# Sparse attention with an FFN: another list of steps for block 0, one exponential for two strided groups, smaller loads of v and q

## The chip, the cores and the metric

The kernel runs on one core of one Trainium2 chip. The metric is the device time of one execution in microseconds (us), as a median of runs. PE is TensorE, DVE is VectorE, ACT is ScalarE, POOL is GpSimd, SP is SyncE, which only issues DMAs here.

## The reference

Eight batches of eight heads, 576 tokens, 64 columns a head, in float32. Heads 0 to 3 attend to the last 32 tokens ("local"), heads 4 to 7 to earlier tokens of the same remainder modulo 32 ("strided"). The result, 4608 tokens of 512 columns, goes through an FFN with a SiLU gate.

```python
rel = pos[:, None] - pos[None, :]
mask_local = (rel >= 0) & (rel < stride)                      # stride = 32
mask_strided = (rel >= 0) & (pos[None, :] % stride == pos[:, None] % stride)
scores = np.where(masks, scale * q @ k.T, -1e9)               # masks by head
attn = np.exp(scores - max); attn = attn / (attn.sum() + 1e-9)
x = attn @ v                                                  # heads side by side
h = x @ w_in                                                  # 512 -> 2048
out = (h * (1.0 / (1.0 + np.exp(-h)))) @ w_out                # 2048 -> 512
```

## The kernel before, in words

**FFN.** The 4608 tokens are nine blocks (k) of 512; the 2048 hidden columns are 16 chunks (fc) of 128. Float32 products are made of a high and a low part each of the operands: for each chunk and block, `hidden` (L617) does twelve products of 128x512 with w_in, `output` (L683) twelve with w_out. The weights' parts are made while block 0 is computed, and stay in SBUF.

**Attention.** A batch is six groups: three local ones of twelve tiles (n = 3 columns of the layout) and three strided ones of 8, 8 and 6 tiles (n = 4, 4, 3). In batch 0 they come in this order, groups 0 to 5; from batch 1 on a local and a strided one in turn. Block 0 needs batch 0, so batch 0's attention stands at the start of the program; two groups later than that (6 to 13) lie inside block 0, and the rest between the chunks of later blocks (`products`, L928), two groups at a time.

**Steps and the list.** The program up to the end of block 0 is a list of steps, written out as text (`PLAN`, L104). `follow` (L163) emits them in the list's order; each engine executes its own instructions in this order, and the semaphores between them follow from what they read and write. A letter after a dot names the engine; without one it is the first of the step's engines. The steps of a group c:

- `kc`: load keys and queries (`load_qk`, L333). In batch 0 this is two DMAs, and for groups 0 to 2 the second one goes through ACT's queue, the others through SP's. Four buffers k0 to k3 serve batch 0, so `k4` waits for S0, `k5` for S1, `k6` for S4. `vc`: load values (L339), in two DMAs on SP.
- `Sc`: scores on PE into two PSUM banks (L384). `Mc`: on DVE, per column and head, minus the scaled and masked score, and its minimum, so that the row's maximum comes out (`peak`, L408). `Ec`: on ACT, one exponential per column and head of 128x64 with the maximum as a bias, and the row sums as a second result (`weigh`, L432). `Rc`: DVE adds 1e-9 and takes the reciprocal (L445).
- `Nc`: multiplies by it (strided groups; DVE or POOL). `Tc`: PE transposes (L460). `Pc`: copies them out of PSUM (ACT or DVE). `Oc`: products with v on PE (L488).
- Local groups go on with `Qc` (DVE divides, L544), `Xc` (PE transposes back, L569) and `Bc` (copy into x); strided ones with `Bc` (sorts into x on ACT, L552).
- From group 6 on, `Vc` (DVE transposes by blocks) takes the place of T and P.

`~n` is n units of 128 columns of products of the identity on PE, without use for the result. `H0c` and `L0c` make the high and low part of x's rows for block 0. A weight's piece i goes through `pi` (load, SP), `ai` (two passes on ACT, L266 and L271), `ji` (DVE, L277), `bi` (high part, DVE or ACT, L318), `di` (low part, DVE or POOL, L322). A chunk fc of block 0 is `h` and `i` (six products each, `hidden`), `t` (tanh, ACT), `g` (DVE), `w` and `l` (high and low part of the gate's output), `o` (twelve products). h0 needs L00, L01 and d0.

**DMAs and semaphores.** DMAs take eight semaphores in turn (DMAHW0 to DMAHW7). A DMA waits until the last one of its own semaphore has landed, on the queue of the engine that issues it, and ACT and SP issue in the order of their instructions.

**Masks.** At the start, POOL builds the local mask of 64 keys and its two variants, those of 96 keys (for the wide form of the scores) and then the strided one (L220 to L240). The wide form (64 queries by 96 keys, half as many products) is used from group 14 on (`WIDE_FROM`).

**End.** `store` (L692) scales the last products out of PSUM, alternately on DVE and ACT, each of 128x512, and SP stores them.

Of the kernel before, what the change touches and what calls it, by code (L numbers as in the profile page):

```python
# [46 lines left out]
WIDE_FROM = 14  # L47
# [8 lines left out]
SPREAD = ()  # L56
# [10 lines left out]
class Group:  # L67
    def __init__(self, local, first, count):
# [4 lines left out]
        self.q0 = [self.rows * t for t in range(count)]  # L73
# [37 lines left out]
N8.D h4 b9.A o1 d9.P t3 g3 h5 M10 p13 E6 p15 v6 b6.D d6.D p12 k7 R6 l2.D o2 a10 j10 a11 j11
b11.D d11.D p17 h6 i4 a8 j8 i5 i6 a13 j13 b13.D w3.A l3.D N6.D V6 b8.A d8.P p14 o3 E10 t4 d13.P
p19 a15 j15 g4 O6 b10.A d10.P p16 t5 g5 h7 b15.D d15.D p21 a12 j12 v8 w4.A l4.D o4 a17 j17
b17.D d17.D p23 R10 i7 w5.A b12.A d12.D p18 a14 j14 a19 j19 B6 t6 g6 S7 k9 h8 l5.D o5 a16 j16
b16.D d16.D p22 V8 k12 M7 i8 t7 g7 O8 h9 v10 N10.P b19.A d19.P w6.A l6.P b14.A d14.D o6 p20 i9
a21 j21 a18 j18 b18.D a23 j23 b23.D w7.A l7.D o7 d23.D p25 a22 j22 b22.D d22.D p24 B8 E7 R7
# [59 lines left out]
def sparse_attention_ffn(ctx: ExitStack, tc: tile.TileContext, kqt, vt, w_in, w_out, out):  # L176
# [44 lines left out]
    for wide, keys in ((False, KW), (True, WIDE)):  # L221
        m = mask(f"mask_local{keys}", keys + 8)
# [4 lines left out]
        masks[wide, ()] = m  # L227
        some = {s for g in GROUPS for s in (g.paired_starts if wide else g.starts) if s}
        for starts in sorted(some):
            first = const.tile([P, keys + 8], F32, name=f"mask{keys}_" + "".join(map(str, starts)))  # L230
            nc.gpsimd.tensor_copy(out=first, in_=m)
            for t in starts:
                keep(first, t * STRIDE, STRIDE, [keys], [1], -STRIDE, 0)
            masks[wide, starts] = first
    m = mask("mask_strided")
# [97 lines left out]
    def load_qk(a):  # L333
        n = max(a.g.nq, a.g.nk)
        ways = (load, nc.scalar.dma_start if a.at < 3 else load)
        for some, way in zip(halved(n, 1 if a.b else 2), ways):
            way(out=kbds[kbd_of(a.b, a.at)][:, :, some], in_=kqt[a.b, a.gi, :, :, some])
# [13 lines left out]
    class Attention:  # L351


        def __init__(self, b, at):
# [24 lines left out]
        def halves(self, banks):  # L379

            n, keys = self.g.n, self.keys
            return [t[:, : n * keys].rearrange("p (c k) -> p c k", k=keys) for t in banks]

        def scores(self, banks=None):  # L384
# [14 lines left out]
            for t, c, rows in self.tiles:  # L399
                for h in range(2):  # L400
                    at = slice(h * D, (h + 1) * D)
                    nc.tensor.matmul(  # L402
                        self.pss[h][rows, c * KW : (c + 1) * KW],
                        kbd[at, 1, g.q0[t] : g.q0[t] + g.rows],
                        kbd[at, 0, g.k0[t] : g.k0[t] + KW], start=True, stop=True,
                    )

        def peak(self):  # L408
# [5 lines left out]
            )  # L414
# [3 lines left out]
            self.inv = rsum.unsqueeze(3).broadcast_to([P, g.n, 2, self.keys])  # L418
            for c in range(g.n):
                for h in range(2):  # L420

                    nc.vector.tensor_tensor_reduce(  # L422
                        out=s_sb[:, c, h], in0=s_ps[h][:, c], in1=self.masks[c][:, : self.keys],
# [4 lines left out]
        def lessen(self):  # L428
            peaks = self.peaks.unsqueeze(3).broadcast_to([P, self.g.n, 2, self.keys])
# [58 lines left out]
        def values(self):  # L488
# [5 lines left out]
            if self.sums_by_pe:  # L494
                for c in range(g.n):
                    at = g.n * D + 2 * c
                    nc.tensor.matmul(
                        self.pso[0][:, at : at + 2], pt[:, c].rearrange("k r q -> k (r q)"), ones,
                        start=True, stop=True,
                    )  # L500
# [210 lines left out]

    def attention_steps(c, due, last=None):
# [6 lines left out]
        cols = max(a.g.nq, a.g.nk)  # L719
        k = add(f"k{c}", {"SP": 2 * P * cols * 4 / RATE}, t0 - 6, [], lambda: load_qk(a),  # L720
# [3 lines left out]
        m = add(f"M{c}", {"DVE": 0.07 + 0.27 * n}, t0 + 1, [s], a.peak, takes=["sm", "sum"],  # L724
# [4 lines left out]
        cost = 0.1 + 0.11 * n if a.spread else 0.667 * n  # L729
# [346 lines left out]
```

## Time and profile before

| | us |
|---|---|
| median of 3 runs | 871.31 (871.29 to 871.56) |
| the profiled execution | 871.88 |
| its span | 870.1 |
| PE busy | 862.5 (99%) |
| DVE busy | 514.1 (59%) |
| ACT busy | 318.7 (37%) |
| POOL busy | 40.3 (5%) |

The profile is one execution: the span goes from the first to the last instruction of the core. PE, DVE, ACT and POOL stand ahead of line, operation, names of the tiles written and read (buffer numbers left out) and sizes; times are us from the span's start, a number in brackets is the engine's idle time ahead of an instruction with what ended it. A 64x64 product of float32 is two matmul records. ACTq and SPq are the queues in which an engine issues DMAs.

### The profile page before, as it was taken

To read this page: it belongs to the slowest core of one execution; us is meant where nothing else is said; L and a number is where in the kernel's file an instruction comes from. 1 tells how busy PE (TensorE), PEld (TensorE's weight loads), DVE (VectorE), ACT (ScalarE), POOL (GpSimd) and SP (SyncE) were. 2 spreads that over 40 slices of the span, in tenths; PEclk is the share of its full clock that TensorE was granted. 3 is DMA by queue.
4 is the path that set the end of the run, shared out by engine and by line. 5 is a ranking of instruction groups with operands and counts; after the bars stand their busy time and mean duration, and the time that the engine had idled before them with its cause. 6 is when DMAs were issued, how large, how long until landed. Compare 5 with 4: busy or idle time off the path is not lost.

```text
span 870.1 us, 17241 instructions
## 1 busy us (share of the span) xinstructions
PE 862.5 (99%) x6809; PEld 707.9 (81%) x6809; DVE 514.1 (59%) x1602; ACT 318.7 (37%) x1070; POOL 40.3 (5%) x68
## 2 busy tenths in 40 slices
PE   8999999999999999999999999999999999999998
PEld 5777788888888888888888888888888888888886
DVE  6999887558556647656655855664762533343333
ACT  7987863315413333333431541333331311131111
POOL 5023320000000000000000000000000000000000
PEclk9999999999999999999999999999999999999999
DMA  9976443202302212220320230221210000000001
GB/s 293 288 251 221 142 157 95 72 2 76 118 1 72 77 50 68 72 77 18 100 73 1 77 117 1 72 76 50 69 29 1 29 20 1 1 27 22 1 1 49
DMA packets 37041, 64.55 MB, mean 74 GB/s; under 512 B 2912, under 2 KB 23776, under 8 KB 36960
## 3 DMA queue, kind: packets, MB, share of 16 engines
q1 hardware_dynamic: 36144, 62.79, 22.3%
q8 instruction: 53, 0.87, 0.4%
q10 hardware_dynamic: 816, 0.66, 0.2%
q14 instruction: 28, 0.23, 0.1%
HBM read 54.00 MB, written 9.44 MB: 73 GB/s over the span
## 4 chain that ended last, share of the span: by engine, by line
PE 92%; DVE 3%; ACT 2%; issue 1%; POOL 1%; POOLq 0%; DVEq 0%; ACTq 0%
PE po L687 44%; PE ps L623 43%; PE ps L526 3%; PE ps L393 1%; PE ps L402 1%; DVE stage L277 1%; DVE sm L422 1%; ACT stage L271 0%; ACT stage L266 0%; POOL mask_local L215 0%; DVE th L655 0%; DVE w L318 0%; ACT xb L566 0%; DVE w L322 0%; ACT sm L439 0%
## 5 line engine op out<-in xcount | busy, mean ns | idle before, releaser
L623 PE MATMUL ps<-xhi,w 128*128 128x512 f32 x1152 | 376.7, 390 | 0.5 <-DVE th L655 0.5
L623 PEld LDWEIGHTS ps<-xhi,w 128*128 128x128 f32 x1152 | 216.2, 188 | 46.0 <-DVE th L655 0.7
L655 DVE SCALAR_TENSOR_TENSOR th<-th,ps 128x512 f32<-128x512 f32 (+1 forms) x147 | 99.2, 675 | 258.6 <-ACT th L633 257.7
L633 ACT ACTIVATE th<-ps 128x512 f32<-128x512 f32 (+1 forms) x147 | 86.7, 590 | 448.3 <-PE ps L623 416.5
L623 PE MATMUL ps<-xlo,w 128*128 128x512 f32 x576 | 224.2, 389 | 0.0
L687 PE MATMUL po<-w,ghi 128*128 128x512 f32 x504 | 156.9, 392 | 0.0
L623 PEld LDWEIGHTS ps<-xlo,w 128*128 128x128 f32 x576 | 108.1, 188 | 22.2
L439 ACT ACTIVATE sm<-sm,sums 128x64 f32<-128x64 f32 (+1 forms) x320 | 109.2, 348 | 2.9 <-DVE sums L422 2.9
L687 PEld LDWEIGHTS po<-w,ghi 128*128 128x128 f32 x504 | 93.7, 188 | 20.0 <-DVE w L322 0.3
L667 DVE TENSOR_TENSOR glo<-th,ghi 128x512 fp32r<-128x512 f32 (+1 forms) x139 | 95.7, 689 | 11.9
L687 PE MATMUL po<-w,glo 128*128 128x512 f32 x252 | 98.4, 390 | 0.4 <-DVE glo L667 0.4
L687 PE MATMUL po<-stage,ghi 128*128 128x512 f32 x288 | 88.8, 389 | 0.0
L486 DVE STREAM_TRANSPOSE pt<-sm 32x192 f32<-32x192 f32 (+1 forms) x168 | 65.8, 392 | 3.0
L687 PE MATMUL po<-v,ghi 128*128 128x512 f32 x216 | 67.5, 394 | 0.0
L663 DVE CAST ghi<-th 128x512 fp32r<-128x512 f32 (+1 forms) x134 | 56.6, 422 | 12.8 <-PE po L687 1.2
L687 PEld LDWEIGHTS po<-stage,ghi 128*128 128x128 f32 x288 | 54.0, 188 | 11.2
L439 ACT ACTIVATION_READ_ACCUMULATOR sm<-sm,sums 128x1 f32 x320 | 61.8, 193 | 0.0
L687 PEld LDWEIGHTS po<-w,glo 128*128 128x128 f32 x252 | 47.3, 188 | 11.1 <-DVE glo L667 1.1
L687 PE MATMUL po<-stage,glo 128*128 128x512 f32 x144 | 56.0, 389 | 0.0
L687 PEld LDWEIGHTS po<-v,ghi 128*128 128x128 f32 x216 | 39.9, 188 | 8.4
L687 PE MATMUL po<-k,ghi 128*128 128x512 f32 x144 | 44.3, 389 | 0.0
L687 PE MATMUL po<-v,glo 128*128 128x512 f32 x108 | 42.0, 389 | 0.0
(77 smaller groups left out, 676.9 us busy)
## 6 DMA issues: line engine op xcount, KB each, us to landing
out<-stage SPq DMA_DIRECT2D x36, 256.0 KB, 2.0
v<-vt SPq DMA_DIRECT2D x21, 384.0 KB, 5.4
stage<-w_out SPq DMA_DIRECT2D x14, 512.0 KB, 4.3
k<-kqt SPq DMA_DIRECT2D x14, 512.0 KB, 4.9
stage<-w_in SPq DMA_DIRECT2D x12, 512.0 KB, 4.4
k<-kqt SPq DMA_DIRECT2D x14, 416.0 KB, 3.9
v<-vt SPq DMA_DIRECT2D x14, 256.0 KB, 5.4
k<-kqt SPq DMA_DIRECT2D x7, 448.0 KB, 3.9
```

Source lines behind the costliest of these rows:

```text
L277: nc.vector.scalar_tensor_tensor(out=upper, in0=upper, scalar=3, in1=lower, op0=ALU.logical_shift_left, op1=ALU.bitwise_or,)
L393: nc.tensor.matmul(self.pss[h][rows, c * WIDE : (c + 1) * WIDE], kbd[at, 1, g.q0[t] : g.q0[t] + 2 * STRIDE], kbd[at, 0, g.k0[t] : g.k0[t] ...
L402: nc.tensor.matmul(self.pss[h][rows, c * KW : (c + 1) * KW], kbd[at, 1, g.q0[t] : g.q0[t] + g.rows], kbd[at, 0, g.k0[t] : g.k0[t] + KW], s ...
L439: nc.scalar.activation(out=self.s_sb[:, c, h], in_=self.s_sb[:, c, h], func=AF.Exp, bias=self.peaks[:, c, h : h + 1], scale=-1.0, accum_ou ...
L486: nc.vector.transpose(out=pt[to, r % 2], in_=src[rows, 1 if self.wide else 1 - r % 2])
L526: nc.tensor.matmul(self.pso[p][h * D : (h + 1) * D, i * size : (i + 1) * size], vbd[at, 2 * i + h], moved, start=True, stop=True,)
L623: nc.tensor.matmul(ph, weight(0, wi, fc)[:, cc * P : (cc + 1) * P], x[xi][cc], start=(cc, n) == (0, 0), stop=(cc, n) == (NP - 1, 2),)
L633: nc.scalar.activation(out=th[:, cols], in_=ph[:, cols], func=AF.Tanh, scale=0.5)
L655: nc.vector.scalar_tensor_tensor(out=th[:, cols], in0=th[:, cols], scalar=1.0, in1=ph[:, cols], op0=ALU.add, op1=ALU.mult,)
L663: copy[engine](out=g[0][:, cols], in_=th[:, cols])
L667: either[engine].tensor_sub(out=g[1][:, cols], in0=th[:, cols], in1=g[0][:, cols].bitcast(F32))
L687: nc.tensor.matmul(po[tt], g[gi][:, cols], weight(1, wi, fc), start=fc == 0 and n == 0, stop=fc == NFC - 1 and n == 2,)
```

## The change

**Steps.** (1) Groups 3 and 4 are in `SPREAD`: a new step `U` on POOL subtracts the maxima from all 128x512 (`lessen`), `E` is one exponential of 128x512 without sums, and `R` begins with a sum on DVE. (2) Groups 0 to 2 are `SHARED`: as neighbouring local tiles share half of their values, only the second half of v's rows is loaded, and a new step `C` on POOL copies the first half from it, within SBUF. (3) Queries of strided groups are packed 59 columns apart instead of 64, and batch 0 loads keys and queries as two DMAs, each with the columns it needs, the queries of groups 0 to 2 through ACT's queue. (4) From group 12 on (`WIDE_FROM`) local scores are wide and strided ones take 54 keys instead of 64 (`seen`), for which POOL sets the rest to zero. (5) The wide masks are built later, in a step `Y0` on POOL, and the strided mask comes third. (6) The very last store is halved: DVE and ACT scale a half each, SP and ACT store one each. (7) Block 0 has a new list.

```diff
-WIDE_FROM = 14
+WIDE_FROM = 12
+SHARED = (0, 1, 2)
-SPREAD = ()
+SPREAD = (3, 4)
-        self.q0 = [self.rows * t for t in range(count)]
+        self.q0 = [(STRIDE if local else STRIDE + HALF) * t for t in range(count)]
 PLAN = """
-k0 k1 k2 k3 v0 ~9 S0 M0 k4 v1 E0 ~1 S1 k5 M1 E1 v2 ~1 S2 M2 E2 R0 ~2 T0 P0.D p0 S3 M3 E3 ~3 T1
...
+k0 k1 v0 C0 v1 ~7 S0 ~1 S1 M0 E0 ~6 T0 P0.A k2 k4 M1 E1 v2 S2 k3 O0 R0 M2 E2 C1 R1 Q0 S4 C2 k5
...
     def load_qk(a):
-        n = max(a.g.nq, a.g.nk)
-        ways = (load, nc.scalar.dma_start if a.at < 3 else load)
-        for some, way in zip(halved(n, 1 if a.b else 2), ways):
-            way(out=kbds[kbd_of(a.b, a.at)][:, :, some], in_=kqt[a.b, a.gi, :, :, some])
+        to, of = kbds[kbd_of(a.b, a.at)], kqt[a.b, a.gi]
+        if a.b:
+            n = max(a.g.nq, a.g.nk)
+            load(out=to[:, :, :n], in_=of[:, :, :n])
+            return
+        load(out=to[:, 0, : a.g.nk], in_=of[:, 0, : a.g.nk])
+        way = nc.scalar.dma_start if a.at < 3 else load
+        way(out=to[:, 1, : a.g.nq], in_=of[:, 1, : a.g.nq])
     def load_v(a):
+        to, of = vbds[vbd_of(a.b, a.at)], vt[a.b, a.gi]
+        if a.shared:
+            for h in range(2):
+                rows = slice(h * KW + STRIDE, (h + 1) * KW)
+                load(out=to[rows, :n], in_=of[rows, :n])
+            return
+    def share_v(a):
+        to = vbds[a.at]
+        for h in range(2):
+            first, second = (slice(h * KW + i * STRIDE, h * KW + (i + 1) * STRIDE) for i in range(2))
+            if a.at == 0:
+                nc.gpsimd.memset(to[first, 0], 0.0)
+            else:
+                nc.gpsimd.tensor_copy(out=to[first, 0], in_=vbds[a.at - 1][second, a.g.count - 1])
+            nc.gpsimd.tensor_copy(out=to[first, 1 : a.g.count], in_=to[second, : a.g.count - 1])
+            self.seen = SEQ if not g.local and b * NG + at >= WIDE_FROM else self.keys
...
-                        self.pss[h][rows, c * KW : (c + 1) * KW],
+                        self.pss[h][rows, c * self.seen : (c + 1) * self.seen],
...
+            if self.seen < self.keys:
+                pad = self.sm[:, : g.n * 2 * KW].rearrange("p (c k) -> p c k", k=KW)
+                nc.gpsimd.memset(pad[:, :, self.seen :], 0.0)
...
+            if (k, tt) == (NBLK - 1, NTT - 1):
+                r0 = k * T + tt * P
+                for some, engine in zip(halved(DM, 2), (nc.vector, nc.scalar)):
+                    if engine is nc.vector:
+                        nc.vector.tensor_scalar_mul(osb[:, some], po[tt][:, some], 0.5)
+                        nc.sync.dma_start(out=out[r0 : r0 + P, some], in_=osb[:, some])
+                    else:
+                        nc.scalar.mul(out=osb[:, some], in_=po[tt][:, some], mul=0.5)
+                        nc.scalar.dma_start(out=out[r0 : r0 + P, some], in_=osb[:, some])
+                continue
...
+    wide_masks = add("Y0", {"POOL": 4.3}, 25.0, [], lambda: fill_local(True))
```

In the new list nearly all of the steps `d` and `l` in block 0 have no letter, which means DVE (before, eleven `d` and eight `l` were POOL's); 25 steps `b` are ACT's, where there were 12, and 7 are DVE's, where there were 20.

Where the instructions stand, for three places. First ACT's queue at the start, before (the exponentials are those of groups 0 to 5, up to the first weight; `k_82` is group 2's buffer):

```order
L337 DMA k_80<-kqt 128x2x208
L337 DMA k_81<-kqt 128x2x224
L337 DMA k_82<-kqt 128x2x208
L439 ACT_TABLE_LOAD
L439 ACTIVATE sm,sums<-sm,sums 128x64 [waits DVE_49] x40
L582 COPY xb<-po 128x3x4x32 [waits PE_49]
L266 ACTIVATE stage_352<-stage_352 128x512 [waits DMAHW3_49,DMAHW2_49]
```

and the same queue in the changed kernel:

```order
L339 DMA k_80<-kqt 128x384
L339 DMA k_81<-kqt 128x384
L463 ACT_TABLE_LOAD
L463 ACTIVATE sm,sums<-sm,sums 128x64 [waits DVE_49] x6
L492 COPY pt<-po 128x384 [waits PE_49]
L339 DMA k_82<-kqt 128x384 [waits DMAHW3_49]
L463 ACTIVATE sm,sums<-sm,sums 128x64 [waits DVE_49] x12
L492 COPY pt<-po 128x384 [waits PE_49]
```

The load of group 2's queries has moved from the start to behind E0 and P0, and it waits for DMAHW3. Second, SP's queue in the changed kernel, where the same semaphore is found (`v_78` is v2's buffer here, `k_80` is now k4's):

```order
L337 DMA k_82<-kqt 128x416 [waits DMAHW0_49]
L337 DMA k_80<-kqt 128x442 [waits DMAHW1_49,PE_49]
L339 DMA k_80<-kqt 128x477 [waits DMAHW2_49]
L347 DMA v_78<-vt 32x768 [waits DMAHW3_49]
L347 DMA v_78<-vt 32x768 [waits DMAHW4_49]
L337 DMA k_83<-kqt 128x442 [waits DMAHW5_49]
```

The first half of v2 counts on DMAHW3 after k1's keys, and the queries of group 2 come third on it, so they wait for both. Before, v2 was loaded in 128 rows, and k2 at the start. Third, PE's queue ahead of the first FFN product, before (L402 are scores, L464 transposes, L511 products with v of strided groups, the last row of 28 is O4 and O5, L623 is h0):

```order
L573 MATMUL po<-ident,xq 128x128 x3
L402 MATMUL ps<-k_80 32x64 x24
L464 MATMUL po<-ident,sm 128x128 x4
L511 MATMUL po<-pt,v_78 64x54 x16
L464 MATMUL po<-ident,sm 128x128 x3
L511 MATMUL po<-pt,v_79 64x54 x28
L623 MATMUL ps<-xhi,w_0_657 128x512
```

and in the changed kernel, from X2 on:

```order
L590 MATMUL po<-ident,xq 128x128 x3
L488 MATMUL po<-ident,sm 128x128 x7
L423 MATMUL ps<-k_80 32x64 x24
L528 MATMUL po<-pt,v_78 64x54 x16
L528 MATMUL po<-pt,v_79 64x54 x12
L423 MATMUL ps<-k_81 64x64 x16
L640 MATMUL ps<-xhi,w_0_647 128x512
```

The scores of groups 8 (x24) and 7 (the last x16) now stand ahead of h0; before, they stood among the products of block 0.

More of the change, by code (lines that the diff above doesn't have):

```diff
@@ L111 @@
[L111 to L116, printed above, removed]
@@ L124 @@
+L12 p31 a31 j31 b31.D o13 o14 w15.A l15 d31 E13 R13 N13 V13
 """
@@ L221, in sparse_attention_ffn, with fill_local @@
     for wide, keys in ((False, KW), (True, WIDE)):
-        m = mask(f"mask_local{keys}", keys + 8)
+        for starts in sorted({s for g in GROUPS for s in (g.paired_starts if wide else g.starts)}):
+            name = f"mask{keys}_" + "".join(map(str, starts))
+            masks[wide, starts] = const.tile([P, keys + 8], F32, name=name)
+    masks[None, ()] = const.tile([P, 72], F32, name="mask_strided")
+    const.tile([P, 168], F32, name="pad1")
+    def fill_local(wide):
+        keys, m = WIDE if wide else KW, masks[wide, ()]
+        nc.gpsimd.memset(m, 0.0)
         for t in range(P // STRIDE):
@@ L226, in sparse_attention_ffn @@
             keep(m, t * STRIDE, STRIDE, [keys], [-1], STRIDE + ahead, 1)
[L227 to L235, printed above, removed]
+        for (kind, starts), first in masks.items():
+            if kind == wide and starts:
+                nc.gpsimd.tensor_copy(out=first, in_=m)
+                for t in starts:
+                    keep(first, t * STRIDE, STRIDE, [keys], [1], -STRIDE, 0)
+    fill_local(False)
+    m = masks[None, ()]
+    nc.gpsimd.memset(m, 0.0)
     for t in range(P // STRIDE):
@@ L358, in __init__ @@
             self.spread = b * NG + at in SPREAD
-            self.sums_by_pe = self.spread and g.local and not self.by_blocks
+            self.sums_by_pe = False
             self.kbd, self.vbd = kbds[kbd_of(b, at)], vbds[vbd_of(b, at)]
@@ L493, in values @@
                 self.pso = self.bank("pso")
[L494 to L500, printed above, removed]
             for t, c, rows in self.tiles:
@@ L723, in attention_steps @@
         steps.reads(s, k_place)
-        m = add(f"M{c}", {"DVE": 0.07 + 0.27 * n}, t0 + 1, [s], a.peak, takes=["sm", "sum"],
+        m = add(f"M{c}", {"DVE": 0.07 + (0.31 if a.wide else 0.27) * n}, t0 + 1,
+                [s, wide_masks] if a.wide else [s], a.peak, takes=["sm", "sum"],
                 gives=[s])
@@ L739, in attention_steps @@
         if last != "S":
-            v = add(f"v{c}", {"SP": P * a.g.count * D * 4 / RATE}, t2 - 5, [],
+            rows = P // 2 if a.shared else P
+            v = add(f"v{c}", {"SP": rows * a.g.count * D * 4 / RATE}, t2 - 5, [],
                     lambda: load_v(a), writes=[v_place])
+            if a.shared:
+                v = add(f"C{c}", {"POOL": 2.2}, t2 - 4, [v] + ([steps[f"v{c - 1}"]] if c else []),
+                        lambda: share_v(a))
+                for i in (c - 1, c)[c == 0 :]:
+                    steps.reads(v, f"v{i}")
         if a.by_blocks:
```

59 lines of the change are left out of this document (27 added, 32 removed).

## Prediction

> **What bounds the kernel now.** I read the stretches by time first, then each engine's instructions in order of time at the start and around the waits, and last the DMA issues. One row of the stretches (PE, PEld, DVE, ACT, POOL busy, clock, DMA share, GB/s):
>
> ```profile
> 200.00:400.00 200.00, 200.00 (x1604) 165.87 (x1603) 125.40 (x403) 68.50 (x260) 0.00 (x0) 1.00 0.19 61
> ```
>
> TensorE never pauses there, so nothing that only relieves VectorE, ScalarE or GpSimd in the later stage can show. Three things count: when the first FFN product (step h0) starts, what TensorE executes or waits for behind it, and the last store. TensorE's order of time gives the first:
>
> ```profile
> 24.07 0.55 PE L464 MATMUL po<-ident,sm 128*128 128x128 f32 x3
> 24.55 1.84 PE L511 MATMUL po<-pt,v 64*64 64x54 f32 x56
> 26.32 0.50 PE L623 MATMUL ps<-xhi,w 128*128 128x512 f32 x1
> ```
>
> T5, O4 and O5 lead straight into h0 at 26.32, and the 870.1 - 26.32 = 843.8 us behind it are products one after the other, but for short waits. So the sum is: the new start of h0, less what leaves the stretch behind it.
>
> **The start: one load decides it.** In the new list the queries of group 2 are still the third load on ScalarE's queue, but they stand behind E0 and P0 there, and the semaphore on which they count is also that of v2's first half, which must have landed. ScalarE executes in order, so everything behind the DMA waits with it. First S0 and M0 of before, and SP's issue of the two halves of k4:
>
> ```profile
> 5.51 0.87 PE L402 MATMUL ps<-k 64*32 64x64 f32 x48
> ```
> ```profile
> 6.59 0.23 DVE L422 CUSTOM_DVE_ANT_0 sm<-ps,mask 128x64 f32<-128x64 f32 x1 [6.59 <-PE ps L402]
> ```
> ```profile
> 6.39 1.21 SPq L337 DMA_DIRECT2D k<-kqt  x2
> ```
>
> Then the DMA issues: the first by ScalarE, and two rows of the first 13 us (out<-in, queue, count, size, median us from issue to landing):
>
> ```profile
> k<-kqt ACTq DMA_DIRECT2D x1, 208.0 KB, 4.0
> ```
> ```profile
> v<-vt SPq DMA_DIRECT2D x6, 192.0 KB, 4.3
> ```
> ```profile
> k<-kqt ACTq DMA_DIRECT2D x1, 224.0 KB, 4.4
> ```
>
> k0 is issued at 0.74 and lands 4.0 later. Two of nine units of filler ahead of S0 go, so S0 can start at 4.75, 0.76 earlier than now, and ends 0.87 later, at 5.6. k4 takes k0's buffer, so SP issues it then; both halves take 1.21, and v2's first half is issued at 6.85. At 4.3 it lands at 11.15. ScalarE is at the DMA sooner: P0 ended at 10.66 (VectorE's idle 1.08 ahead of 11.74, a row below) with S0 0.76 later. So the landing counts: issue at 11.15, and 4.4 to the next landing, **S2 at 15.6**, where now it stands ahead of T0 and the run of O0. Bounds: 4.0 for both loads give 14.9; the three rows differ by 0.4, and half a microsecond more for each load gives 16.6. I take the values between, as these rows come from the same first stretch with its full queues.
>
> TensorE's queue holds O0, S4, T1, S3 and all later steps behind S2; VectorE's holds M2. SP's load k6 waits for S4 and holds v3, p0 and v4 behind it.
>
> **From S2 to h0.** VectorE runs M2 R1 Q0 M4 M3 Q1 R2 M5 B1 R4 N4. Its rows:
>
> ```profile
> 11.74 0.22 DVE L422 CUSTOM_DVE_ANT_0 sm<-ps,mask_strided 128x64 f32<-128x64 f32 x1 [1.08 <-POOL mask_strided L215]
> ```
> ```profile
> 12.90 0.55 DVE L468 COPY pt<-po 128x384 f32<-128x384 f32 x1
> 13.37 0.16 DVE L454 TENSOR_SCALAR sums<-sums 128x6 f32<-128x6 f32 x1
> 13.57 0.19 DVE L455 RECIPROCAL sums<-sums 128x6 f32<-128x6 f32 x1
> 13.67 0.58 DVE L550 TENSOR_TENSOR xq<-po,sums 128x192 f32<-128x192 f32 x2
> ```
> ```profile
> 24.89 0.69 DVE L322 TENSOR_TENSOR w<-stage,w 128x512 fp32r<-128x512 f32 x1
> 25.50 0.42 DVE L318 CAST w<-stage 128x512 fp32r<-128x512 f32 x1
> ```
>
> Start to start, the eight maxima of a strided M take 1.16 (11.74 to 12.90), so six take 0.87; a copy of 384 columns (B1) 0.47, R 0.30, Q 0.50 (its 0.58 less the 0.08 by which an end overlaps the next start), an operation of 128x512 with two operands 0.61. The new sum over 128x512 is in no row; its price lies between the cast's 0.42 and the two-operand row's 0.69, and I take 0.60, near the latter, whose output is as precise and whose input as long. From S2's start to M2's I take 1.08, as from S0's to M0's. Then 0.87 + 0.30 + 0.50 + 1.16 + 1.16 + 0.50 + 0.30 + 0.87 + 0.47 + (0.60 + 0.30) + 0.61 = 7.64 to the end of N4. T4 with four transposes takes 0.7 (0.55 with three). Then ScalarE's order is P4 H00 a0 B4 P3 B2 P5 H01. Its rows:
>
> ```profile
> 22.50 0.59 ACT L468 COPY pt<-po 128x512 f32<-128x512 f32 x1
> 22.97 0.71 ACT L266 ACTIVATE stage<-stage 128x512 f32<-128x512 f32 x1
> 23.55 0.71 ACT L271 ACTIVATE stage<-stage 128x512 int32<-128x512 uint32 x1
> 24.65 0.48 ACT L468 COPY pt<-po 128x384 f32<-128x384 f32 x1 [0.40 <-PE po L464]
> 25.03 2.29 ACT L566 COPY xb<-po 128x432 f32<-128x432 f32 x4
> 27.35 0.62 ACT L599 CAST xhi<-xb 128x512 fp32r<-128x512 f32 x1
> 27.88 0.69 ACT L266 ACTIVATE stage<-stage 128x512 f32<-128x512 f32 x1
> ```
>
> P4 0.47, H00 0.53, a0 twice 0.58, B4 0.9 (two of the four copies that fill 25.03 to 27.35), P3 0.47, B2 and P5 0.38 each, H01 0.53: 4.82. Last, L01 is GpSimd's:
>
> ```profile
> 36.09 1.31 POOL L667 TENSOR_TENSOR glo<-th,ghi 128x512 fp32r<-128x512 f32 x1 [14.99 <-ACT ghi L663]
> ```
>
> It takes 1.31, with two hand-overs 1.41. In all 1.08 + 7.64 + 0.7 + 4.82 + 1.41 = 15.65: **h0 at 31.25, 4.93 later than now**. A second lane ends beside it: P4 is done 9.9 behind S2's start, and then O4, X2, T3, T5, S8, O3, O5 and S7 stand ahead of h0 on TensorE: 1.77 for O4 and O5 (24.55 to 26.32), 1.05 for O3, 0.5 each for X2, T3 and T5, 0.6 each for S8 and S7, 5.5 together. So a faster single step would gain little; the landing in front of S2 moves both lanes.
>
> What lies beside these lanes and costs nothing: GpSimd's subtractions, by the row of N3 below, since U4 can start 3.9 behind S2, ends at 5.0, and its exponential has until R4 at 7.2.
>
> ```profile
> 17.60 1.04 POOL L458 TENSOR_TENSOR sm<-sm,sums 128x512 f32<-128x512 f32 x1 [5.45 <-ACT sm L439]
> ```
>
> If U4 took 1.5 longer, R4 would be late by the rest. The copies of C0 to C2, two of 704 columns each, take at most 1.4 apiece by this row's 1.04 for 512, 8.4 in all from the end of the strided mask; O2 needs the last of them 7 behind S2, so they are over. The strided mask, done earlier, frees the 1.08 at 11.74, and the shorter exponentials free ScalarE; both gains now lie inside the wait for S2. The smaller loads are already in v2's issue at 6.85.
>
> **Behind h0.** S8 and S7 have left this stretch for the time ahead of h0:
>
> ```profile
> 32.80 0.39 PE L623 MATMUL ps<-xlo,w 128*128 128x512 f32 x1
> 33.03 0.39 PE L623 MATMUL ps<-xhi,w 128*128 128x512 f32 x1
> 33.34 0.72 PE L402 MATMUL ps<-k 64*32 64x64 f32 x48
> 34.00 0.50 PE L623 MATMUL ps<-xhi,w 128*128 128x512 f32 x1
> 34.34 0.40 PE L623 MATMUL ps<-xlo,w 128*128 128x512 f32 x1
> ```
> ```profile
> 65.83 0.39 PE L623 MATMUL ps<-xhi,w 128*128 128x512 f32 x1
> 66.15 0.69 PE L402 MATMUL ps<-k 64*64 64x64 f32 x32
> 67.36 0.50 PE L623 MATMUL ps<-xhi,w 128*128 128x512 f32 x1 [0.51 <-DVE th L655]
> 67.69 0.39 PE L623 MATMUL ps<-xlo,w 128*128 128x512 f32 x1
> ```
>
> Two products take 0.46 (32.80 to 33.03, doubled). S8 costs 34.34 - 33.03 - 0.46 = 0.85; S7 costs 67.69 - 65.83 - 0.46 = 1.40, of which 0.51 is a wait: 0.89 without it. Together -1.74. The wait I leave in the sum, since another wait of that kind can stand elsewhere in the new list; it may be gone (-0.51), or there may be more (the third rival). Group 12's scores become wide, half as many products: between nothing and half of a 0.66 us run (33.34 to 34.00), taken as -0.1. The strided scores of batches 2 to 7 lose ten of 64 columns. Three stretches of one burst in the later stage, in products of 32, of 54 and of 64 columns:
>
> ```profile
> 230.11:230.40 0.29, 0.29 (x34) 1.00 0.00 0
> 230.83:231.12 0.29, 0.29 (x32) 1.00 0.00 0
> 231.30:231.60 0.29, 0.29 (x32) 1.00 0.00 0
> ```
>
> 0.29 us holds 34, 32 and 32 of them: the pace doesn't go by columns, so this is worth nothing. The last store is halved:
>
> ```profile
> 866.41 0.60 ACT L701 ACTIVATE stage<-po 128x512 f32<-128x512 f32 x1 [0.76 <-PE po L687]
> ```
>
> At best half of it and a little of the transfer go: between nothing and -0.5, taken as -0.2.
>
> **The sum**, against the profile's own span: 870.1 + 4.93 - 1.74 - 0.1 - 0.2 = 873.0, 2.9 more. The profiled execution took 871.88 with its span of 870.1, the median of the runs is 871.31; with the same 2.9 that becomes **874.2 us**.
>
> **The rivals.**
>
> 1. *S2 is not held* (faster). If the queries land soon enough for S2 to follow T0 at about 10, the freed ScalarE and the earlier mask decide: h0 at 10 + 15.65 = 25.7, the sum 870.1 - 0.6 - 2.04 = 867.5, the time 868.7. It breaks even with S2 at 12.7. For it: ScalarE's order alone would let the DMA go at 9.9. Against it: then 4.0 are still to come, and v2's landing before it. Chance 0.06.
> 2. *The hold is short and block 0 smooth* (same). S2 at 14.9 or a lane half a microsecond shorter, and the 0.51 gone: 2.9 - 0.7 - 0.5 - 0.5 = +1.2, 872.5. Were the score runs to go by columns after all, 18 runs of 0.6 would each lose a tenth of a microsecond: 1.8 less, 872.4. Chance 0.22.
> 3. *VectorE becomes the bound in block 0* (slower still). Nineteen subtractions move from GpSimd to VectorE there, 19 x 0.61 = 11.6, thirteen casts move to ScalarE, 13 x 0.42 = 5.5 less, and the work begins 5 us later. If a quarter of the 6.1 shows as waits: 875.7. Chance 0.14.
> 4. *TensorE cools while it waits for S2.* A run of 48 took 0.87 at the start, and 0.66 at 33.34. If the runs S2, O0, S4, S3 and O1 are each 0.2 longer, Q1 waits for O1 and h0 is up to 1.0 later: 875.2. Chance 0.08.
>
> The rule for the last: the Trainium skill, page "TensorE: Matmul & The Clock Gate", part 1 on the clock gate, says that TensorE goes back to half its clock after an idle window of some 3.4 us and needs about as long of work to leave it. The row at 5.51 agrees for a cold start; no trace here shows a second cooling.
>
> **How the numbers follow.** The forecast has 0.50. A measurement of this kernel can tell about 0.2%, 1.74 us, from no change: 869.57 to 873.05. Faster 0.06; same 0.22; slower 0.50 + 0.14 + 0.08 = 0.72. The range leaves out rival 1 and the ends of rivals 2 and 3: low 871.6 (rival 2 with another lane shortened), high 876.8 (S2 at 16.6 and rival 3 together).
>
> **What would show it.** Right: S2 near 15.6, released by a load of k; VectorE idle from about 8 to 16; h0 near 31; strided score runs as long as before. Wrong: S2 ahead of 13, or an h0 that is late behind another step than S2, or more than 2 us of waits behind h0.

## The result, and the profile after

The changed kernel takes 876.35 us (875.34 to 878.26), where the one before took 871.31 (871.29 to 871.56): 1.0059 times as long, 95% interval 1.0047 to 1.0072. Its profiled execution took 876.03, its span is 874.2, 4.1 more than before. The four runs spread over 2.9, those of before over 0.3.

The instructions around the wait for S2, in order of time (ScalarE's issue and next exponential, TensorE, VectorE):

```profile
11.28 0.34 ACTq L339 DMA_DIRECT2D k<-kqt  x1
11.66 0.35 ACT L463 ACTIVATE sm<-sm,sums 128x64 f32<-128x64 f32 x1 [2.40 <-DMA v<-vt]
15.48 1.07 PE L423 MATMUL ps<-k 64*32 64x64 f32 x48 [6.73 <-DMA k<-kqt]
16.57 0.23 DVE L446 CUSTOM_DVE_ANT_0 sm<-ps,mask__93 128x64 f32<-128x64 f32 x1 [7.71 <-PE ps L423]
```

ScalarE stands for 2.40, released by a load of v; only then is the third DMA issued, at 11.28, and S2 starts at 15.48, released by a load of k. TensorE is idle for 6.73 and VectorE for 7.71. That is the forecast hold, at the forecast place.

What came with it is in TensorE's stretches of 3.41 us, laid so that the granted clock changes only at their ends (PE busy, granted clock, DMA share, GB/s):

```profile
5.86:9.27 3.41, 2.89 (x57) 1.00 0.94 263
9.27:12.69 3.42, 0.00 (x0) 1.00 0.96 290
12.69:16.10 3.41, 0.62 (x38) 0.50 0.49 169
16.10:19.51 3.41, 3.41 (x125) 0.50 0.02 5
19.51:22.92 3.41, 3.13 (x143) 1.00 0.84 247
```

From 12.69 to 19.51 the clock is 0.50. S2's run took 1.07 where the same 48 records took 0.72 to 0.73 later.

Two more things lie between S2 and h0. GpSimd's second subtraction and VectorE's small addition beside it:

```profile
21.77 1.04 POOL L454 TENSOR_TENSOR sm<-sm,sums 128x512 f32<-128x512 f32 x1 [0.75 <-PE po L523]
22.00 0.83 DVE L478 TENSOR_SCALAR sums<-sums 128x6 f32<-128x6 f32 x1
```

The addition over 128x6 ends with GpSimd's operation and took 0.83 instead of 0.16. And TensorE, just ahead of h0:

```profile
30.59 1.61 PE L528 MATMUL po<-pt,v 64*64 64x54 f32 x48
33.48 0.32 PE L528 MATMUL po<-pt,v 64*64 64x54 f32 x5 [1.28 <-issue]
...
34.32 0.50 PE L640 MATMUL ps<-xhi,w 128*128 128x512 f32 x1
```

In the middle of O5 it stops for 1.28, released by nothing that the profile shows. h0 starts at 34.32, 8.00 later than before. Behind it the stretch is 839.9 instead of 843.8. TensorE's waits there, before:

```profile
PE ps L623 <- DVE th L655: 0.5, 1, 0.5
PE po L687 <- DVE glo L667: 0.4, 1, 0.4
```

The same view of the changed kernel from 34.3 on has no row.

### The profile page after: what moved, and what is told of

Same layout as the page of the kernel before. It is cut to its first block, busy times and chain, and to the rows that moved or that the text cites. A ratio compares the mean times of both kernels' runs of the same rounds, so it can differ in the third digit from the quotient of the medians.

```text
span 874.2 us, 17209 instructions
## 1 busy us (share of the span) xinstructions
PE 859.4 (98%) x6779; PEld 707.4 (81%) x6779; DVE 513.0 (59%) x1609; ACT 322.3 (37%) x1058; POOL 24.7 (3%) x75
## 4 chain that ended last, share of the span: by engine, by line
PE 97%; DMA 1%; DVE 1%; issue 0%; ACT 0%; SPq 0%; POOL 0%; POOLq 0%; ACTq 0%
PE po L704 45%; PE ps L640 45%; PE ps L543 3%; PE ps L423 2%; PE ps L414 1%; DMA v<-vt 1%; DMA k<-kqt 0%; PE ps L817 0%; PE po L528 0%; PE po L488 0%; PE po L523 0%; PE po L590 0%; DVE sums L478 0%; DVE sm L446 0%; DVE sm L482 0%
## 5 line engine op out<-in xcount | busy, mean ns | idle before, releaser
L684 DVE TENSOR_TENSOR glo<-th,ghi 128x512 fp32r<-128x512 f32 (+1 forms) x147 | 99.8, 681 | 11.8
L463 ACT ACTIVATE sm<-sm,sums 128x54 f32<-128x54 f32 (+2 forms) x304 | 103.0, 345 | 8.6 <-DVE sums L446 6.2
L463 ACT ACTIVATION_READ_ACCUMULATOR sm<-sm,sums 128x1 f32 x304 | 58.5, 192 | 0.0
```

The lines of the kernel that those rows point to most:

```text
L463: nc.scalar.activation(out=self.s_sb[:, c, h], in_=self.s_sb[:, c, h], func=AF.Exp, bias=self.peaks[:, c, h : h + 1], scale=-1.0, accum_ou ...
L684: either[engine].tensor_sub(out=g[1][:, cols], in0=th[:, cols], in1=g[0][:, cols].bitcast(F32))
```

## Experiments

All were timed beside the kernel before (medians of 871.32 to 871.40). "Theory A" is the prediction's: the hold of S2 is what the change costs. Where a line shows "issue" as the releaser, the profile shows nothing that the engine waited for.

### The hold taken away, in two ways

```diff
-k0 k1 v0 C0 v1 ~7 S0 ~1 S1 M0 E0 ~6 T0 P0.A k2 k4 M1
+k0 k1 k2 v0 C0 v1 ~7 S0 ~1 S1 M0 E0 ~6 T0 P0.A k4 M1
```

> The changed kernel with one word of its list moved: k2 stands third, ahead of v0, so that ScalarE issues group 2's queries as its third instruction, ahead of E0 and P0. Theory A (the hold of S2 by that load is what the change costs): S2 follows T0 at 9 to 10 us instead of 15.48, TensorE's clock stays at 1.00, h0 comes 17 later, at 26 to 27 instead of 34.32, and with about 840.5 behind it the time is 868 to 870, faster than before (871.31). Rival B (the new list is slow by its own lanes on VectorE and ScalarE, whatever S2 does): S2 is early, but h0 stays above 31 and the time at 873 or more.

```diff
-        way = nc.scalar.dma_start if a.at < 3 else load
+        way = nc.scalar.dma_start if a.at < 2 else load
```

> The changed kernel with group 2's queries sent through SyncE's queue instead of ScalarE's, at the same place of the list, so that no engine that computes stands in front of them. Theory A: issued at about 4.8, landing 4 to 5 later, S2 at 9 to 10, time 868 to 871; k4 and all loads behind it on SyncE start 0.4 later. Rival B as above: 873 or more. Rival C (it is the place in the list, not the queue: the loads ahead of it fill the queues until 13 us): S2 at 12 to 14, time 872 to 874.

The first took 873.42 (871.62 to 875.71; ratio 1.0023, 1.0013 to 1.0033), the second 873.32 (870.84 to 874.91; 1.0015, 1.0006 to 1.0024). TensorE in the first:

```profile
8.81 0.72 PE L423 MATMUL ps<-k 64*32 64x64 f32 x48
...
17.36 0.34 PE L423 MATMUL ps<-k 64*64 64x64 f32 x6 [2.21 <-issue]
...
28.80 0.32 PE L528 MATMUL po<-pt,v 64*64 64x54 f32 x5 [1.80 <-issue]
29.65 0.50 PE L640 MATMUL ps<-xhi,w 128*128 128x512 f32 x1
```

S2 is at 8.81 in the first and at 8.21 in the second, so rival C fell, and 2.9 and 3.0 of the 5.0 are gone: the hold is shown to be a cause. The rest of theory A fell. The times lie above its 868 to 871, h0 comes at 29.65, not 26 to 27, and TensorE waits twice with "issue" as the releaser, in the middle of S5 and of O5; the second kernel has the same two waits, of 1.91 and 1.10, and h0 at 29.50. Rival B, which had the time right (873 or more), fell with its condition: h0 is well ahead of 31. The stretches around the second wait of the first kernel:

```profile
26.62:30.03 3.41, 1.61 (x56) 1.00 0.99 371
30.03:33.45 3.42, 3.42 (x10) 0.50 0.95 308
```

A stretch in which TensorE was busy for 1.61 of 3.41 is followed by one at half the clock, though no single wait in it is longer than 1.80; the first products of block 0 run in it.

The waits stand where a count says. Stretches from the start to just ahead of them, with the numbers of instructions (PE, PEld, DVE, ACT, POOL), in this kernel, and then up to the one such wait of before (0.61, in O3):

```profile
0.00:17.35 17.35, 13.43 (x344) 8.92 (x344) 8.44 (x78) 11.07 (x45) 13.42 (x42) 1.00 0.90 284
0.00:28.80 28.80, 22.21 (x595) 15.78 (x596) 19.25 (x134) 20.06 (x70) 16.48 (x46) 1.00 0.90 291
```
```profile
0.00:23.06 23.06, 20.15 (x473) 13.28 (x473) 14.52 (x109) 16.82 (x86) 11.49 (x46) 1.00 0.94 295
```

That is 688, 1191 and 946 products and weight loads; with the 16 to 27 other records of TensorE's queue in the trace they are, within two, the 706th, the 1218th and the 962nd instruction, 256 apart or 512. In the trace each such wait ends 1.2 to 1.5 after the end of a packet of 16 KB on the queue of kind "instruction". When TensorE executes the first instruction of one block of 256, the packet with the next follows after a lag:

| kernel (times in us) | 450th instruction | packet starts | lag | share of DMA time that loads took meanwhile | 706th |
|---|---|---|---|---|---|
| before | 11.88 | 13.80 | 1.92 | 0.98 | 17.80, no wait |
| changed | 17.63 | 18.19 | 0.56 | 0.00 | 21.66, no wait |
| k2 first | 10.70 | 15.03 | 4.33 | 1.00 | 17.36, after 2.21 |
| k2 by SyncE | 11.64 | 15.45 | 3.82 | 0.85 | 17.68, after 1.91 |

So the changed kernel had no wait in S5 because the hold had emptied the queues, and two more kernels with the hold (a warm TensorE and R2 ahead of GpSimd's subtraction, both below, with lags of 0.93 and 0.45) have none there either. The hold hid one fetch of instructions; a later one met full queues and came late (962nd at 27.98, packet at 31.23, the 1.28 at the 1218th). The Trainium skill, page "Runtime: NRT & Kernel Launch", section "Instruction fetch mechanics", says that an engine's instructions are refilled in blocks of 16 KiB, 256 of them, over a DMA queue of its own while the present block is executed, and that the cost is mostly hidden. The count agrees; hidden it is not here, with 0.6 to 3.4 at a boundary.

### The hold alone, in the old list

```diff
-k0 k1 k2 k3 v0 ~9 S0 M0 k4 v1 E0 ~1 S1 k5 M1 E1 v2 ~1 S2
+k0 k1 k3 v0 ~9 S0 M0 k4 v1 E0 ~1 S1 M1 v2 k2 k5 E1 ~1 S2
```

> The kernel before, with only the loads of group 2 moved: k2 stands behind v2 instead of third, so its queries are issued by ScalarE behind E0 and its keys by SyncE behind k4 and v2 (k5 follows it). Theory A: S2 comes at 14 to 16 instead of 7.91, TensorE cools in front of it, h0 comes 5 to 7 later than 26.32, and the time is 875 to 879. Rival D (block 0 absorbs a late S2 in the old list, since other lanes end later): 871 to 873.

It took 879.14 (878.09 to 880.46; ratio 1.0087, 1.0074 to 1.0100):

```profile
14.73 0.96 PE L402 MATMUL ps<-k 64*32 64x64 f32 x48 [6.60 <-DMA k<-kqt]
...
32.51 0.50 PE L623 MATMUL ps<-xhi,w 128*128 128x512 f32 x1
```

S2 is 6.8 later than before, h0 6.2, the time 7.8, just above the range of theory A. A late load of group 2 is enough for a loss in the old list too; rival D fell.

### A warm TensorE

```diff
-M1 E1 v2 S2 k3 O0
+M1 E1 v2 ~26 S2 k3 O0
```

> The changed kernel with 26 units of filler on TensorE (about 5.7 us at full clock) between T0 and S2, nothing else changed. S2 stays at 15.5, since its load does. Theory E (the cold clock costs part of the 3.2 by which the way from S2 to h0 was longer than worked out): the clock stays at 1.00, S2 and O0 take 0.7 to 0.8 instead of 1.07 and S4 0.7 instead of 1.13, VectorE's waits of 0.21 and 0.26 ahead of M4 and M3 go, h0 comes 0.4 to 1.0 earlier, time 875.4 to 876.0. Rival F (VectorE's order sets the pace anyway): 876.3, no change.

It took 875.50 (875.00 to 876.16; ratio 1.0044, 1.0032 to 1.0056), 0.85 less than the changed kernel, in intervals that overlap. One stretch and four rows of TensorE:

```profile
12.14:15.55 3.41, 1.97 (x6) 1.00 0.77 262
```
```profile
15.97 0.82 PE L423 MATMUL ps<-k 64*32 64x64 f32 x48 [1.86 <-DMA k<-kqt]
...
26.70 0.80 PE L817 MATMUL ps<-ident 128*128 128x384 f32 x2 [1.15 <-issue]
32.75 0.73 PE L528 MATMUL po<-pt,v 64*64 64x54 f32 x18 [1.09 <-issue]
33.99 0.50 PE L640 MATMUL ps<-xhi,w 128*128 128x512 f32 x1
```

The clock stays at 1.00. From S2's start to N4's end it is 8.8 instead of 10.6: the cold clock and the addition beside GpSimd (0.16 here, where it began at 21.33, 0.04 ahead of GpSimd's subtraction) cost 1.8 of that lane. But h0 is only 0.33 earlier: what the lane gained went into two waits for instructions, at the 962nd and the 1218th. The products of filler put the second one 28 instructions earlier in the steps, at the same count.

### S8 and S7 behind h0

```diff
-j1 b0.D L00.D d0 p2 v6 B2.A S8 M8 p4 P5.A
+j1 b0.D L00.D d0 p2 v6 B2.A p4 P5.A
-v7 S7 M7 k9 a5
+v7 a5
-p6 k10 h0 h1 i0 i1 t0 g0 h2 h3 i2 t1 g1 w0.D
+p6 h0 h1 i0 i1 t0 g0 h2 h3 i2 t1 g1 S8 M8 k10 w0.D
-S10 a11 j11 b11.D t3 g3 d11
+S7 a11 j11 b11.D t3 g3 M7 k9 d11
-t4 g4 h6 M10 O6
+t4 g4 h6 S10 M10 O6
```

> The kernel of e1_k2_first with S8, M8, S7 and M7 (and k10, k9) put back behind h0: S8 behind g1, S7 in the place of S10, S10 behind h6. Theory G (TensorE's instructions come in blocks of 256, weight loads and products counted together; in every trace so far the waits without a releaser stand at the 706th, 962nd or 1218th, and while the queues of the loads are full a block takes 4 to 7 us): the 1218th instruction now lies some 80 behind h0, among products of 0.23, so the wait of 1.80 in O5 is gone and none takes its place; that at the 706th, in S5, stays at about 2. h0 comes at 26.5 to 27.5 instead of 29.65, no stretch at half clock follows it, behind h0 it is 841.5, time 869.8 to 871. Rival H (the wait in O5 is one of O5's own, for its values or a bank): it stays, h0 at 28.3 or later, time 871.5 to 873.

It took 880.16 (876.95 to 881.67; ratio 1.0097, 1.0082 to 1.0113); the profiled execution is its fastest. h0 started at 27.11, with no wait for instructions in O5 or at the 1218th: theory G held and rival H fell. The waits that are left ahead of h0 stand at the 706th (1.85) and, for the first time, at the 450th (0.75). The time went the other way. VectorE's and TensorE's waits behind h0:

```profile
37.91 0.23 DVE L446 CUSTOM_DVE_ANT_0 sm<-ps,mask 128x64 f32<-128x64 f32 x1 [2.21 <-PE ps L423]
49.18 0.23 DVE L446 CUSTOM_DVE_ANT_0 sm<-ps,mask_strided 128x64 f32<-128x64 f32 x1 [1.36 <-PE ps L423]
51.68 0.73 PE L640 MATMUL ps<-xhi,w 128*128 128x512 f32 x2 [1.89 <-DVE w L320]
```

VectorE stands in front of M8 and M7, TensorE later for a low part that VectorE had not made. Behind h0 it is 848.1. The follow-up moves ten low parts to GpSimd:

```diff
-d9 ... l1 ... d13 ... d8 ... d10 ... d12 ... l5 ... d16 ... d14 ... l6
+d9.P ... l1.P ... d13.P ... d8.P ... d10.P ... d12.P ... l5.P ... d16.P ... d14.P ... l6.P
```

> The kernel of e5_s78_back (880.16) with the same ten low parts on GpSimd. There TensorE waited 5 to 6 us behind h0 for VectorE. If VectorE's work is what is too much (rival 3 of the prediction, once h0 is early): 10 x 0.69 less, time 873.5 to 876. If it is the order (VectorE stands in front of M8, M7 and M10 for 5.4 us and can't go on): 878.5 to 880.5.

879.10 (877.85 to 880.71; ratio 1.0088, 1.0074 to 1.0101), not to be told from 880.16. Behind h0 the two traces have 848.0 and 848.1, and VectorE still stands 4.3 in front of the maxima of M8, M7 and M10, where it was 5.4. So less work on VectorE did not help, which points to the order; no run moved these steps alone.

### The one exponential undone

The base is the kernel with k2 first; the sums are the exponentials' own again.

```diff
-SPREAD = (3, 4)
+SPREAD = ()
-v4 U4 E4 S5 v5 R2 U3 M5
+v4 E4 S5 v5 R2 M5
```

> The kernel of e1_k2_first without the first part of the change: groups 3 and 4 get eight exponentials of 128x64 with a bias and a sum again, no step U on GpSimd and no sum on VectorE. If the one exponential is worth something on the path: ScalarE's lane is 2 x 2.07 longer ahead of P4, N4 waits for E4, h0 is 0.5 to 2 later, time 874 to 875.5. If its price on VectorE (the sum, 0.85 a group, and 0.7 to 0.9 in which a small operation there stood beside GpSimd's subtraction) is as large as its gain, or both are hidden behind TensorE's waits: 873.4 as e1, within 0.5; if the price is the larger: 872 to 873.

874.80 (873.10 to 876.98; ratio 1.0037, 1.0025 to 1.0050), against 873.42. ScalarE's copy P4, here and in the base:

```profile
23.79 0.57 ACT L492 COPY pt<-po 128x512 f32<-128x512 f32 x1
```
```profile
21.79 0.59 ACT L492 COPY pt<-po 128x512 f32<-128x512 f32 x1 [1.63 <-PE po L488]
```

In the base ScalarE waits 1.63 for it; here it comes without a pause behind 22 exponentials of 0.33 that started at 16.50, and so 2.0 later than in the base. The one exponential is worth that much of ScalarE's lane where S2 is not held. What it is worth in time is less sure: the times hardly separate the two, and while h0 is 1.9 later (31.55), the wait for instructions in S5 was 3.01 here and 2.21 in the base.

### Two small parts in the old list

```diff
-WIDE_FROM = 14
+WIDE_FROM = 12
```

and the halved last store, as in the change.

> The kernel before with two parts of the change that need no new list: WIDE_FROM = 12 and the halved last store. By the bursts in the traces of before and after (group 12's scores and the products beside them cost 0.36 less, the last store 0.04): 870.9, 0.4 less. If wide scores are worth half of a score run as well and half the store's 0.6 goes: 870.5. If they are worth nothing: 871.3.

871.36 (871.33 to 872.43; ratio 1.0000, 0.9991 to 1.0009): worth nothing. Group 12's scores cost 0.86 between two products in either form. The 0.36 of the expectation was a misreading of the two traces. Before, these scores stand alone between two large products (0.97 from the start of the one to that of the next) and O7's products in one run with another group's (1.62); in the changed kernel they share a run with O7's (1.43), and the other group's stand alone (1.15). Together it is 2.6 in both.

### R2 ahead of GpSimd's subtraction

```diff
-a1 O1 Q1 v4 U4 E4 S5 v5 R2 U3 M5
+a1 O1 R2 Q1 v4 U4 E4 S5 v5 U3 M5
```

> The changed kernel with R2 moved ahead of Q1 in the list, so that VectorE does it before GpSimd subtracts the maxima of group 3. Theory I (the 0.83 of R2's first operation, where 0.16 to 0.17 is usual, is a wait for GpSimd's subtraction beside it, and VectorE's lane from S2 to N4 sets T4): R2 takes 0.3, N4 ends 0.6 to 0.7 earlier than 26.04 + 0.69, the block at the 1218th instruction is fetched as much earlier, time 875.6 to 875.8. Rival J (another operation beside U3 is stretched instead, or the lane has slack): N4 within 0.2 of before, time 876.3.

876.11 (875.26 to 880.28; ratio 1.0062, 1.0046 to 1.0078), no change. VectorE:

```profile
21.07 0.17 DVE L478 TENSOR_SCALAR sums<-sums 128x6 f32<-128x6 f32 x1
21.27 0.19 DVE L479 RECIPROCAL sums<-sums 128x6 f32<-128x6 f32 x1
22.00 0.62 DVE L567 TENSOR_TENSOR xq<-po,sums 128x192 f32<-128x192 f32 x2 [0.54 <-PE po L523]
```

The addition takes 0.17, so the 0.83 was GpSimd's doing. But VectorE now waits 0.54 for O1, and N4 ends 0.2 earlier than in the changed kernel: rival J.

### Fewer instructions ahead of h0, and smaller loads

```diff
-            self.wide = g.local and b * NG + at >= WIDE_FROM
+            self.wide = g.local and b * NG + at >= TURNED
-R2 U3 M5 ... p27 Y0 t9
+R2 U3 Y0 M5 ... p27 t9
```

(TURNED is 6; the base is the kernel with k2 first.)

> The kernel of e1_k2_first with wide scores for all local groups from group 6 on (24 products and 24 weight loads instead of 48 and 48), and Y0 moved up in the list behind U3, since M6 now needs the wide mask. S6 and S8 stand ahead of h0, so 96 of TensorE's instructions are gone there, and the 1218th is one of chunk 0's first products. Theory G (blocks of 256 instructions): the wait of 1.80 in O5 is gone, that in S5 at the 706th stays at about 2, S6 and S8 are 0.3 shorter each; h0 comes at 27 to 27.7 instead of 29.65. If VectorE keeps up behind h0, it is 839.8 behind it, time 868.5 to 869.5. Rival K (VectorE and ScalarE are full behind h0 and only hid that as long as h0 was late): the waits for them return, and the time stays at 871 to 873.5.

872.25 (870.54 to 874.01; ratio 1.0010, 1.0001 to 1.0019):

```profile
18.42 0.48 PE L423 MATMUL ps<-k 64*64 64x64 f32 x6 [3.02 <-issue]
30.46 0.47 PE L640 MATMUL ps<-xhi,w 128*128 128x512 f32 x1
```
```profile
14.69:18.10 3.41, 0.71 (x33) 1.00 0.96 308
18.10:21.52 3.42, 3.10 (x81) 0.50 0.52 175
21.52:24.93 3.41, 3.41 (x24) 0.50 0.67 215
```

The wait in O5 is gone; its remainder, 0.66, stands at the same count, which is now the second product of h1. The wait in S5 was 3.02 in this execution, and two stretches at half clock followed, so h0 came at 30.46. The forecast h0 was not met. The time lies in rival K's range, but what K names did not come (no wait for VectorE behind h0). The count was met.

The same ten low parts on GpSimd in this kernel:

```diff
-d9 ... l1 ... d13 ... d8 ...
+d9.P ... l1.P ... d13.P ... d8.P ...
```

> The kernel of e9_fewer with eight low parts of weights and... of gates, ten in all (d8, d9, d10, d12, d13, d14, d16, l1, l5, l6), on GpSimd instead of VectorE: 10 x 0.69 off VectorE behind h0. If rival K holds for e9_fewer, its waits behind h0 shrink by up to 6, and the time falls to 868.5 to 870.5; if there is nothing to relieve there, it is that of e9_fewer or up to 1 more, since a low part on GpSimd takes 1.3 instead of 0.69 and chunks wait for it.

876.33 (875.38 to 877.38; ratio 1.0057, 1.0044 to 1.0069), 4.1 more, where at most 1 was expected: there was nothing to relieve. In the traces h0 is 1.0 later (31.42, behind a wait of 3.44 in S5), and behind it stand 843.0 instead of 841.1. TensorE waits 0.3 to 0.5 at four places for VectorE, two of them where blocks are transposed; how the ten steps lead to these was not followed up, so the 4.1 are not explained.

Last, smaller loads on the base of the kernel with fewer instructions:

```diff
-            for some in halved(NP, 2 if i < AHEAD else 1):
+            for some in halved(NP, 4 if i < 4 else 2 if i < AHEAD else 1):
-            for some in halved(2 * DM, 2 if i < AHEAD else 1):
+            for some in halved(2 * DM, 4 if i < 4 else 2 if i < AHEAD else 1):
-            load(out=to[:, :, :n], in_=of[:, :, :n])
+            for some in halved(n, 2 if a.b == 1 and a.at < 3 else 1):
+                load(out=to[:, :, some], in_=of[:, :, some])
```

> The kernel of e9_fewer with the first four pieces of weights loaded in quarters instead of halves, and the loads of groups 6 to 8 in halves: the same bytes in DMAs half as large, of which at most eight are under way. Theory L (a block of instructions waits behind the bytes that are already under way: 0.56 from the 450th instruction to its packet with idle queues, 3 to 5 with full ones): the packet comes 1 to 2 earlier, the wait in S5 at the 706th shrinks from 3.0 to 1 or less, TensorE's clock is not halved behind it, h0 at 27 to 28.5, time 869.5 to 871. Rival M (the block waits for its turn whatever the size of the loads, or SyncE, which issues twice as many, now sets the pace): the wait stays at 2 to 3 or the scores wait for their loads, time 872 to 874.

872.42 (871.31 to 873.05; ratio 1.0009, 1.0000 to 1.0018):

```profile
17.12 0.34 PE L424 MATMUL ps<-k 64*64 64x64 f32 x6 [1.81 <-issue]
28.21 0.47 PE L641 MATMUL ps<-xhi,w 128*128 128x512 f32 x1 [0.19 <-DVE sums L447]
```
```profile
14.95:18.36 3.41, 1.60 (x51) 1.00 0.88 268
18.36:21.77 3.41, 3.41 (x66) 0.50 0.68 193
```

In this execution the lag behind the 450th instruction was 3.64 instead of 4.70 and the wait 1.81 instead of 3.02, still enough for half the clock behind it. h0 came in the range of theory L, but the time did not move, as rival M has it. One trace of each can't say whether the shorter lag is the size of the loads. No version beat the kernel before.

## Why the prediction was right, and where its sum was not

| step (us) | predicted | measured |
|---|---|---|
| S2 starts | 15.6 | 15.48 |
| M2's start to N4's end | 7.64 | 9.47 |
| h0 starts | 31.25 | 34.32 |
| behind h0, against before | -2.04 | -3.86 |
| span, against before | +2.9 | +4.15 |
| median, against before | +2.9 | +5.04 |

**The hold** was right in mechanism, place and size: ScalarE's DMA behind v2's landing, S2 within 0.12. Taking it away gave 2.9 and 3.0 back, where the prediction's rival 1 puts it at 5.5.

**From S2 to h0** the sum was 3.2 too small; this is the step that was mis-sized. 1.8 is VectorE's lane: 0.68 for R2 beside GpSimd, 0.25 for R4, whose sum takes 0.68 instead of the 0.60 that I took, and most of the rest waits for TensorE ahead of M4, M3 and Q1 (0.21, 0.26 and 0.18). Those are rival 4, which I gave 0.08 and a price of 1.0: the clock was halved for 6.8. The prediction says that no trace shows a second cooling; that of before does, at its end, where the clock is 0.50 from 869.71 on, behind a stretch with 0.02 of work. The last 1.06 is O5's wait for instructions beyond the lane that I followed to L01, which ended at 33.26. Hand-overs make up the other 0.3. So h0 was not "near 31", one of the prediction's signs of being right, and it was late behind another step as well as S2. The wait for instructions was in no term and no rival, although the trace of before has one, in O3, that the prediction passes over:

```profile
23.06 1.07 PE L511 MATMUL po<-pt,v 64*64 64x54 f32 x29 [0.61 <-issue]
```

**Behind h0** I had left the wait of 0.51 in the sum, and beside S8 and S7 taken only 0.1 for group 12 and 0.2 for the end. S8 and S7 gave 1.74 as worked out. The wait of 0.51 went as well, two waits for the low part of a gate gave 1.0, waits in the runs of O6 and O8 0.4, the end 0.04, and group 12 nothing. The two waits are these of TensorE's weight loads before (together, times, longest); the products behind them came 0.76 and 0.2 late:

```profile
PEld po L687 <- DVE glo L667: 1.1, 2, 0.7
```

In the changed kernel h0 is 8 later, and the other engines had that much longer to get ahead of TensorE. The runs don't prove that this is why the waits went. The kernel of the new list whose h0 came earliest (27.11) is one that has waits for VectorE back, but it has S8 and S7 back in this stretch too. So rival 3, VectorE as the bound, did not come, for as long as h0 was late.

**Narrower columns** are worth nothing, as forecast. The same run in a burst, of 64 columns before and of 54 now:

```profile
231.18 0.66 PE L402 MATMUL ps<-k 64*64 64x64 f32 x32
```
```profile
140.91 0.65 PE L423 MATMUL ps<-k 64*64 64x54 f32 x32
```

All 17 bursts together gained 0.14. **The last store** was to give 0.2 and gave 0.04, because its halves follow each other: ScalarE's half waits for VectorE's.

```profile
870.55 0.42 DVE L718 TENSOR_SCALAR stage<-po 128x256 f32<-128x256 f32 x1
871.06 0.38 ACT L721 ACTIVATE stage<-po 128x256 f32<-128x256 f32 x1 [1.22 <-DVE stage L718]
```

**Rival 1** (S2 not held, 868.7) could be tried: with S2 at 8.81 the time was 873.4. It had the same gap as the sum, since h0 at S2 plus 15.65 takes for granted that TensorE gets its instructions.

So the mechanism was right, and that the number came out within its range was in part luck. Two errors of opposite sign (+3.2 from S2 to h0 and -1.8 behind it), with the -0.1 of S2, left the forecast span 1.25 short. The other 0.9 of the 2.2 between forecast and median is that the two profiled executions don't lie on their medians: that of before is 0.57 above, that of the changed kernel 0.32 below.

**Open** stays, in part, why the times of the kernels with the new list spread over 1.2 to 5.0 where those of before spread over 0.3 to 1.2. Two things on record bear on it. The first is the mean granted clock of each execution, which a single stretch of 3.41 at half clock lowers by 0.002. The executions of before kept 0.999 or more and those with a warm TensorE 0.997 or more, and these spread least (1.2). With k2 by SyncE the five executions at 0.997 or more took 870.8 to 872.8, the six at 0.996 or less 873.3 to 874.9. It is not all of it: the five of the kernel with fewer instructions and ten low parts on GpSimd all had 0.996 and spread over 2.0. The second is that a wait for instructions can come in one execution and not in another. Up to h0 the kernel with the two small parts is the kernel before; in its trace nothing waits in O3, and h0 is at 25.46 instead of 26.32. No two executions of one kernel with the new list were profiled.

## What to carry to other kernels

A DMA issued by a computing engine starts when that engine's stream and the DMA's semaphore let it (here it stopped ScalarE for 2.40 and left TensorE idle for 6.73); where a list moves such a DMA behind computing steps, look for who needs it before anything else is costed. In a stretch of many small products under full DMA queues, count TensorE's instructions in 256s against the time between boundaries, and look for waits with no releaser in the middle of a step. A list that frees one engine early is worth what the next limit allows, and here a wait in front had been hiding that limit.

## What the runs showed of the hardware that was not expected

- TensorE's queue stops at a 256th instruction whose block has not come: 0.61 (before), 1.28 (changed), 2.21 and 1.80 (k2 first), 1.91 and 1.10 (k2 by SyncE), 1.15 and 1.09 (a warm TensorE), 0.75 and 1.85 (S8 and S7 behind h0), 3.02 and 0.66 (fewer instructions), 1.81 (smaller loads). From the 450th, 706th or 962nd instruction to the packet with the next block it was 0.45 to 0.93 with idle queues (four kernels) and 1.2 to 5.9 with loads under way.
- The clock goes by stretches of 3.41 on a fixed grid. In the first 35 us it was halved behind all ten, over these kernels, in which TensorE was busy for 1.61 or less (0.00 to 1.61), and not behind those with 1.71, 1.78 and more. It came back behind ten stretches with 3.32 or more, and stayed halved behind those with 0.00, 0.62, 2.39, 2.74 and 3.10; how full a stretch must be is not settled more closely than that, as at the start of three executions the first full clock on record follows a stretch with 3.0 to 3.1. The Trainium skill, page "TensorE: Matmul & The Clock Gate", Part 1, section "What's actually happening", gives a free-running window of 3413 ns and half the clock after an idle window. The length agrees; a window less than half busy was enough here.
- A small addition on VectorE (128x6) beside a GpSimd operation over 128x512 in SBUF took 0.83 instead of 0.16 and ended with it; maxima that read PSUM beside the first such operation kept their 0.145 from start to start.
